# Value products over two steps, and the hash in even steps from two products and an addition

## The chip, the cores and the metric

One core of a Trainium2 chip. TensorE (PE) multiplies, with a queue of its own for weight loads (PEld); VectorE (DVE), ScalarE (ACT) and GpSimd (POOL) work on tiles in SBUF; TensorE writes to PSUM; SyncE (SP) issues most transfers. The metric is the device time of one launch in microseconds (us); a lower one is better.

## The reference

```python
# q, k, v: (4, 8, 768, 64); proj: (64, 6); w_in: (512, 2048); w_out: (2048, 512); all float32
q_bits, k_bits = (q @ proj > 0), (k @ proj > 0)          # 6 bits: a bucket per row
mask = q_bucket[:, :, :, None] == k_bucket[:, :, None, :]
scores = np.where(mask, scale * q @ k.T, -1e9)
attn = softmax(scores)                                    # sum + 1e-9 below the line
x = (attn @ v).transpose(0, 2, 1, 3).reshape(3072, 512)
h = x @ w_in
out = (h * np.clip(h + 3, 0, 6) / 6) @ w_out
```

Attention over 32 heads (4 batches of 8), in which a query meets only the keys of its own hash bucket, and then a dense network over 3072 tokens.

## The kernel before

Every float32 operand is split into a high part in the matrix unit's own format (F32R) and the rest, the low part; a product is a sum of products of parts. So a head's hash is a sum over q and k of high and low parts with the projection's high and low parts, and its signs become bits that stand as extra rows beside q and k in the score product (`hash_qk`, `bits`).

A *step* k handles one block of 128 queries of a head (6 steps a head, 192 in all), in a software pipeline: step k makes the scores of block k+3 (`lead`, tile `s`), the row minimum of block k+2 (`lowest`, VectorE, L396), its exponential (ScalarE, L408) and its transpose in 32x32 blocks (`flip`, VectorE, L429). The transpose is finished by a round trip through DRAM (`move`): the block comes back into the buffer `spare` for even blocks and `px` for odd ones. From there `split_p` makes the high parts `ph` (ScalarE, L475) and the low parts `pl`, for two halves of the keys, c = 0 and c = 1: the low part of c = 0 is a subtraction on VectorE (L479), that of c = 1 one on GpSimd (L477). Two blocks share one pair of tiles; a new pair of blocks begins in an odd step, with the block that lies in `spare`. The tiles lie in rings of two per tag, one turn for c = 1 and one for c = 0:

```python
both = [sp.tile([P, ...], F32R, name=f"{x}{u}_{c}", tag=x, bufs=2)[:, :S] for x in ("ph", "pl")]
```

so a pair's tiles are those of the pair before, and are free when that pair's value products have read them. The value products (`values_whole`, tile `acc`, L513) are 12 matmuls of a pair, six over `ph` and six over `pl`, in an odd step.

From step 102 on (`GT`; `paced`) each step also runs one of 16 slices of the dense network for a chunk of 256 tokens: the first dense product (`gemm1`, tile `h`, 12 matmuls, L661), the gate (ScalarE L683, VectorE L684) and the second dense product of the slice before (`gemm2`, tile `po`, 6 matmuls, L699, L700, L704), which needs the gate's high part (ScalarE, L689) and, last, its low part (VectorE, L690: `gb` or `ga`). The order on PE, DVE, ACT and POOL is written out by hand: `beside_ffn` calls the pieces, and the generator `ffn` is resumed at the marks A to D. So every engine works through its instructions in the order of the code. In a step of this stage TensorE does, in this order: the value products (odd steps), the first dense product, the hash (once in six steps), the second dense product, the scores. VectorE does the minimum, the gate's low part, the block transpose, the gate's product, the subtraction for `pl`, and what the hash needs. `hash_qk` runs in a step k with (k+3) % 6 == 4, which is odd.

Accumulators `acc`, `h`, the hash's `z` and the transposed reciprocals `rt` share four banks of PSUM (`bank`, tags `pt` and `pu` in turn, two each): a new tile waits for the last reader of the tile whose bank it is given. The score tile has one buffer in this stage. The hash's operands are row groups of a head: `k2` and `q2` hold high and low parts, made by copies over DMA (`moves`, one a step) and subtractions on GpSimd (`subs`).

Of the kernel before, what the change touches and what calls it, by code (L numbers as in the profile page):

```python
# [43 lines left out]
def lsh_attention_moe(  # L44
# [75 lines left out]
    pjh = cp.tile([P, ZM + ZK - D], F32R, name="pjh")  # L120
    nc.vector.memset(pjl[:].bitcast(F32), 0.0)
    nc.vector.memset(pjh[:].bitcast(F32), 0.0)
    pjk, pjq = pjh[:, :ZM], pjh[:, ZK - D :]

# [9 lines left out]
    nc.vector.memset(three[:], 3.0)  # L134

# [99 lines left out]
    def get_qk(i: int, tag: str = "raw"):  # L235
        b, h = divmod(i, H)
        if tag == "raw":
            raws[i] = sp.tile([P, S], F32, name=f"raw{i}", tag=tag, bufs=1)[:]
        else:
            raws[i] = wide_tile([P, 2 * WC], F32, f"raw{i}")[:, :S]  # L240
        if paced:
            dma(out=raws[i][:D], in_=qkT[b, h, :D])
        else:
            dma(out=raws[i], in_=qkT[b, h])

    def get_k_rows(i: int):
        b, h = divmod(i, H)
        moves.append(lambda: dma(out=raws[i][D:], in_=qkT[b, h, D:]))
# [6 lines left out]
    def hash_weights():  # L255
# [3 lines left out]
        for r, c in ((slice(0, D), D), (slice(D, P), ZK)):  # L259
            pos = pjh[r, ZK + NB : ZM]  # L260
            nc.vector.tensor_sub(pjl[r, c + NB : c + 2 * NB], pr[r], pos.bitcast(F32))
            nc.vector.tensor_sub(pjl[r, c : c + NB], pos.bitcast(F32), pr[r])

# [16 lines left out]
    moves = []  # L280
# [44 lines left out]
    def hash_qk(i: int):  # L325
        k1, k2, q1, q2 = state[i]
        if paced:
            z = zs[i] = [bank([P, HW], f"z{i}_{j}") for j in range(2)]
        else:
            both = pair(f"z{i}")  # L330
            z = zs[i] = [both[:, j, :HW] for j in range(2)]
# [5 lines left out]
        if not paced:  # L337
            zs[i] = both

    def bits(i: int):  # L340
# [3 lines left out]
        if isinstance(z, list):  # L344
            whole = [(slice(j * HW, (j + 1) * HW), z[j][D:ZM], False) for j in range(2)]
        elif i == 0:
# [144 lines left out]
    def values(u: int, c: int):  # L491
# [5 lines left out]
        for part, y in enumerate((hi, lo)):  # L497
            for x in range(QT):
# [4 lines left out]
                )  # L503

# [533 lines left out]
    def lead(j: int):  # L1038
# [35 lines left out]
    def value_whole():  # L1074
        nonlocal vnext
        values_whole(vnext // 2)
        vnext += 2

# [20 lines left out]
    with tc.manual_schedule(engines={ET.PE, ET.DVE, ET.Activation, ET.Pool}):  # L1099
# [15 lines left out]
        def beside_ffn(k: int):  # L1115
# [9 lines left out]
            for _ in range(2):  # L1125
                u = vnext // 2
                if u < NS // 2 and (2 * u < GT or k % 2 and k >= 2 * u + 3):
# [8 lines left out]
            behind = (k - 1 + LA) % KT == 4  # L1136
# [48 lines left out]
            if GT <= k + 1 < NS:  # L1185
                move(k + 1)

            place_in_chunk = (k - GT) % NFC
            if subs and (k % 2 and (k < GT or place_in_chunk != NFC - 1) or k > GT and place_in_chunk == 0):
# [5 lines left out]
        for k in range(NS + LT + 2):  # L1195
# [11 lines left out]
            if k == HK:  # L1207
                late["x"] = sp.tile([P, S], F32, name="late", tag="raw", bufs=1)
            for c in range(2):
# [118 lines left out]
```

## Time and profile before

| | |
|---|---|
| median of 3 runs | 976.26 us (974.35 to 977.39) |
| profiled execution | 973.11 us, its span 971.3 us, granted TensorE clock 0.998 |
| busy share | PE 98%, PEld 90%, DVE 74%, ACT 64%, POOL 49% |
| stage with the dense network beside the attention | from 412 to 810 us |
| DMA in that stage | 81% of 16 engines, 239 GB/s |
| after it | dense network alone, from 810 us to the end |

Rows in order of time give start, duration, engine, line, operation, `out<-in` with the shapes, and in brackets the idle time of the engine ahead of the instruction and what ended it. Rows of a stretch give its length and, for PE, PEld, DVE, ACT and POOL, busy us and (instructions), then the clock, the DMA share and GB/s. Rows of waits name who waited for whom: total us, times, the longest.

### The profile page before, as it was taken

The page shows a single profiled execution, that of the slowest core. Times are in us where ns is not written, and L with a number is a line of the kernel's source. Part 1 is how long each engine was busy: PE and PEld are TensorE (multiplying, and loading weights), DVE is VectorE, ACT ScalarE, POOL GpSimd, SP SyncE. Part 2 cuts the span into 40 slices and gives each one's busy share as a digit, 9 for nine tenths or more (in the row PEclk, how much of TensorE's full clock was granted, in tenths as well). Part 3 has the DMA queues.
Part 4 walks back from the last instruction along what each step waited for, and adds up shares of the span by engine and source line. Part 5 has one row for each costly group of instructions (what it writes and reads, how often), then busy time and mean ns, then how long its engine had stood idle before and what let it go on. Part 6 is the DMA issues. An engine that isn't in the chain of part 4 may idle for free.

```text
span 971.3 us, 19460 instructions
## 1 busy us (share of the span) xinstructions
PE 948.0 (98%) x6306; PEld 873.6 (90%) x6306; DVE 723.5 (74%) x1470; ACT 625.0 (64%) x1421; POOL 473.6 (49%) x582
## 2 busy tenths in 40 slices
PE   8999999999999999899999999999999999999997
PEld 7999888999989999799899899989899899889896
DVE  7999988888569999877878878878777874342422
ACT  6898875655478988667766666666666664333332
POOL 6777744665537776455555545555545432000000
PEclk9999999999999999999999999999999999999999
DMA  3567579100035554787898788788887772101000
GB/s 117 140 156 188 131 224 377 58 1 1 6 119 119 115 142 112 192 252 233 238 267 234 231 256 241 230 267 236 243 258 233 211 227 71 44 1 44 1 22 22
DMA packets 113613, 152.06 MB, mean 157 GB/s; under 512 B 13876, under 2 KB 82612, under 8 KB 113512
## 3 DMA queue, kind: packets, MB, share of 16 engines
q1 hardware_dynamic: 108472, 144.79, 48.8%
q0 software_dynamic: 5040, 6.03, 5.3%
q8 instruction: 50, 0.82, 0.4%
q14 instruction: 51, 0.42, 0.2%
HBM read 77.34 MB, written 54.00 MB: 135 GB/s over the span
## 4 chain that ended last, share of the span: by engine, by line
PE 79%; DVE 8%; DMA 4%; ACT 4%; issue 3%; POOL 1%; SPq 1%; ACTq 0%; DVEq 0%; POOLq 0%
PE h L661 25%; PE acc L500 6%; PE po L704 6%; PE po L699 6%; PE po L700 6%; PE acc L513 6%; PE pt L418 5%; PE s L389 5%; PE s L387 5%; DMA spare<-fd 2%; DVE p L396 2%; DVE pl L479 2%; ACT ph L475 1%; SPq L78 1%; DVE qq L352 1%
## 5 line engine op out<-in xcount | busy, mean ns | idle before, releaser
L408 ACT ACTIVATE p<-p,m 128x768 f32<-128x768 f32 x192 | 180.2, 939 | 113.4 <-DVE p L396 105.2
L396 DVE TENSOR_SCALAR_CACHE_REDUCE p<-s 128x768 f32<-128x768 f32 x192 | 182.7, 952 | 24.9 <-PE pt L418 12.4
L684 DVE SCALAR_TENSOR_TENSOR h<-g,h 128x256 f32<-128x256 f32 x192 | 81.1, 423 | 102.0 <-ACT g L683 99.0
L683 ACT ACTIVATE g<-h,three 128x256 f32<-128x256 f32 x192 | 91.2, 475 | 94.9 <-PE h L661 94.0
L661 PE MATMUL h<-xh,w 128*128 128x256 f32 x1024 | 146.8, 282 | 0.0
L661 PEld LDWEIGHTS h<-xh,w 128*128 128x128 f32 x1024 | 134.9, 188 | 4.2 <-ACT xh L650 0.6
L429 DVE STREAM_TRANSPOSE p<-p 128x768 f32<-128x768 f32 x90 | 88.1, 979 | 65.2 <-ACT p L408 65.1
L477 POOL TENSOR_TENSOR pl<-spare,ph 128x384 fp32r<-128x384 f32 x45 | 45.8, 1018 | 127.3 <-ACT ph L475 71.4
L479 DVE TENSOR_TENSOR pl<-pt,ph 128x384 fp32r<-128x384 f32 x196 | 100.0, 550 | 4.0 <-ACT ph L475 3.5
L387 PE MATMUL s<-kk,qq 76*128 76x384 f32 x384 | 100.5, 343 | 2.0 <-ACT kk L357 1.5
L389 PE MATMUL s<-kk,qq 128*128 128x384 f32 x384 | 100.4, 343 | 0.0
L700 PE MATMUL po<-w,gb 128*128 128x512 f32 x250 | 98.4, 393 | 0.0
L699 PE MATMUL po<-w,gb 128*128 128x512 f32 x250 | 98.3, 393 | 0.0
L475 ACT CAST ph<-pt 128x384 fp32r<-128x384 f32 x196 | 86.1, 474 | 14.3 <-PE pt L418 13.0
L216 POOL TENSOR_TENSOR w<-wr,w 128x128 fp32r<-128x128 f32 x128 | 71.9, 593 | 45.2 <-ACT w L210 41.9
L418 PE MATMUL pt<-ident,p 128*128 128x128 f32 x612 | 86.2, 275 | 1.9 <-DVE pl L479 1.1
L689 ACT CAST gb<-h 128x256 fp32r<-128x256 f32 x141 | 52.4, 372 | 54.5 <-DVE h L684 26.8
L661 PE MATMUL h<-xl,w 128*128 128x256 f32 x512 | 81.2, 280 | 0.0
L418 PEld LDWEIGHTS pt<-ident,p 128*128 128x128 f32 x612 | 72.5, 141 | 8.9 <-PE pt L418 1.5
L704 PE MATMUL po<-w,gb 128*128 128x512 f32 x250 | 78.6, 395 | 1.5 <-DVE gb L690 1.5
L318 POOL TENSOR_TENSOR kk<-raw,qq 64x192 fp32r<-64x192 f32 (+1 forms) x73 | 65.4, 920 | 25.1 <-ACT qq L304 21.7
L387 PEld LDWEIGHTS s<-kk,qq 76*128 76x128 f32 x384 | 66.6, 190 | 11.7 <-ACT kk L357 2.0
(153 smaller groups left out, 2150.9 us busy)
## 6 DMA issues: line engine op xcount, KB each, us to landing
fd<-p SPq DMA_DIRECT2D x90, 384.0 KB
spare<-fd SPq DMA_DIRECT2D x180, 96.0 KB
px<-fd SPq DMA_DIRECT2D x180, 96.0 KB
kk<-qq SPq DMA_DIRECT2D x62, 192.0 KB
wr<-in_w_in SPq DMA_DIRECT2D x16, 512.0 KB
wr<-in_w_out SPq DMA_DIRECT2D x16, 512.0 KB
raw<-in_qkT SPq DMA_DIRECT2D x19, 384.0 KB
vr<-in_v SPq DMA_DIRECT2D x32, 192.0 KB
```

Source lines behind the costliest of these rows:

```text
L387: nc.tensor.matmul(s[:, c, :HW], lhsT=q1[:KM, us], rhs=half(k1[:KM], c), start=True, stop=False)
L389: nc.tensor.matmul(s[:, c, :HW], lhsT=q2[:, us], rhs=half(k2, c), start=False, stop=True)
L396: nc.vector.tensor_scalar(out=pr_[:], in0=s[:, :, :HW], scalar1=CAP, scalar2=None, op0=ALU.min, op1=ALU.min, accum_out=m[:],)
L408: nc.scalar.activation(pr_[:], pr_[:], AF.Exp, bias=m[:], scale=-1.0, accum_out=sms[b][:, t, h : h + 1])
L418: nc.tensor.transpose(pt[:, x], probs[g][0][:, c, x * P : (x + 1) * P], ident[:])
L475: nc.scalar.copy(hi, pt)
L479: lows.append(lambda: engine.tensor_sub(lo, pt, hi.bitcast(F32)))
L661: nc.tensor.matmul(hp, lhsT=wi[:, wp, wc], rhs=x[cc][xp], start=(k == 0 and cc == 0), stop=(k == 2 and cc == NCC - 1),)
L683: nc.scalar.activation(r[:], hp, AF.Relu, bias=three[:], scale=1.0)
L699: nc.tensor.matmul(po[u], lhsT=gh[:, us], rhs=wo[:, 0], start=(fc == 0), stop=False)
L700: nc.tensor.matmul(po[u], lhsT=gh[:, us], rhs=wo[:, 1], start=False, stop=False)
L704: nc.tensor.matmul(po[u], lhsT=gl[:, us], rhs=wo[:, 0], start=False, stop=(fc == NFC - 1))
```

## The change

In the stage from step 102 on:

- the value products of a pair are split: the six over `ph` run in the odd step, behind the first dense product (`value_part(k, 0)`), and the six over `pl` at the start of the next even step (`value_part(k, 1)`);
- the hash runs one step earlier, in an even step ((k+3) % 6 == 3), and all waiting `subs` and `moves` are issued ahead of it;
- it is four matmuls for six: weights `pjs` (made once, on GpSimd, in the place of `pjh`) give 24 rows of partial sums in rows 0 to 23 and 24 in rows 96 to 119 of `z`; ScalarE copies the first group into rows 96 to 119 of the next head's `raw` tile, VectorE adds the second, and a third VectorE pass over 24x768 in SBUF compares with the thresholds. Before, two passes over 44x384 in PSUM did it;
- the K rows of the next head are loaded a step later than before (`get_k_rows` at t == 4), since their rows hold the sums until then; this load and the transfer of the k bits go to SP behind the loads of `move`; one of `subs` may go in every step.

```diff
+    def short_weights():
+        pjs = cp.tile([P, ZK + NR + NQ], F32R, name="pjs", tag="pjh")
+        nc.gpsimd.memset(pjs[:].bitcast(F32), 0.0)
+        short.extend([pjs[:, : ZK + NR], pjs[:, NQ:]])
...
     def hash_qk(i: int):
         k1, k2, q1, q2 = state[i]
         if paced:
-            z = zs[i] = [bank([P, HW], f"z{i}_{j}") for j in range(2)]
+            zs[i] = []
+            for j in range(2):
+                c = slice(j * HW, (j + 1) * HW)
+                z = bank([P, HW], f"z{i}_{j}")
+                zs[i].append(z)
+                nc.tensor.matmul(z[: ZK + NR], lhsT=short[1], rhs=q2[:, c], start=True, stop=False)
+                nc.tensor.matmul(z[: ZK + NR], lhsT=short[0], rhs=k2[:, c], start=False, stop=True)
+            return
...
     def bits(i: int):
...
         if isinstance(z, list):
-            whole = [(slice(j * HW, (j + 1) * HW), z[j][D:ZM], False) for j in range(2)]
+            r = slice(ZK, ZK + NR)
+            if i + 1 not in raws:
+                raws[i + 1] = sp.tile([P, S], F32, name=f"raw{i + 1}", tag="raw", bufs=1)[:]
+            both = raws[i + 1][r]
+            for j in range(2):
+                nc.scalar.copy(both[:, j * HW : (j + 1) * HW], z[j][:NR])
+            for j in range(2):
+                c = slice(j * HW, (j + 1) * HW)
+                nc.vector.tensor_add(both[:, c], z[j][r], both[:, c])
+            nc.vector.tensor_scalar(
+                out=q1[D : D + NR], in0=both, scalar1=ths[r], scalar2=vas[r], op0=ALU.is_gt, op1=ALU.mult,
+            )
+            behind_home.append(lambda: dma(out=k1[D : D + NQ].bitcast(F32), in_=q1[D + NQ : D + NR].bitcast(F32)))
+            return
...
+    def values_part(u: int, part: int):
+        vv = vvs[2 * u // KT]
+        if part == 0:
+            accs[u] = bank([P, 2 * P], f"acc{u}")
+        acc = accs[u]
+        for c in (1, 0):
+            y = parts[u, c][part]
+            for x in range(QT):
+                nc.tensor.matmul(
+                    acc[:], lhsT=vv[:, c * QT + x], rhs=y[:, x],
+                    start=(part, c, x) == (0, 1, 0), stop=(part, c, x) == (1, 0, QT - 1),
+                )
...
-                if paced:
-                    get_k_rows(n + 1)
+        if t == 4 and paced and n + 1 < NJ and n != H + 1:
+            get_k_rows(n + 1)
...
+            value_part(k, 1)
-            behind = (k - 1 + LA) % KT == 4
+            behind = (k - 1 + LA) % KT == 3
             if GT <= k < NS - 2 and not behind:
                 lowest(k + 2)
             go("A")
...
             if split:
                 split_p(k - LT, 1, False)
             go("B")
+            value_part(k, 0)
...
-            hashed = k + LA < NS and (k + LA) % KT == 4 and (k + LA) // KT + 1 < NJ
+            hashed = k >= GT and k + LA < NS and (k + LA) % KT == 3 and (k + LA) // KT + 1 < NJ
             if hashed:
+                while subs:
+                    subs.pop(0)()
+                while moves:
+                    moves.pop(0)()
                 hash_qk((k + LA) // KT + 1)
...
             if GT <= k + 1 < NS:
                 move(k + 1)
+            while behind_home:
+                behind_home.pop(0)()
```

TensorE around the hash of head 27, before (odd step 157; `acc77` the value products, `h2_0_7` the first dense product, `z27` the hash, `gb2_0_6` the gate of the step ahead):

```order
L387 MATMUL s159_8997<-kk_26_8435,qq_26_8436 128x384 x2
L389 MATMUL s159_8997<-kk_26_8435,qq_26_8436 128x384 x2
L513 MATMUL acc77_9007<-ph77_1_8913,vv25_8705 128x256 x3
L513 MATMUL acc77_9007<-ph77_0_8939,vv25_8705 128x256 x3
L513 MATMUL acc77_9007<-pl77_1_8914,vv25_8705 128x256 x3
L513 MATMUL acc77_9007<-pl77_0_8940,vv25_8705 128x256 x3
L661 MATMUL h2_0_7_9034<-xh2_0_8572,w14_2678 128x256 x8
L661 MATMUL h2_0_7_9034<-xl2_0_8573,w14_2678 128x256 x4
L334 MATMUL z27_0_9047<-qq_27_8825,pjl_74 108x384
L335 MATMUL z27_0_9047<-kk_27_8824,pjh_75 108x384
L336 MATMUL z27_0_9047<-qq_27_8825,pjh_75 108x384
L334 MATMUL z27_1_9048<-qq_27_8825,pjl_74 108x384
```

and now (even step 156, with the low half of the pair ahead, `acc76`, at its start):

```order
L429 MATMUL s158_8965<-kk_26_8452,qq_26_8453 128x384 x2
L553 MATMUL acc76_8945<-pl76_1_8806,vv25_8723 128x256 x3
L553 MATMUL acc76_8945<-pl76_0_8839,vv25_8723 128x256 x3
L716 MATMUL h2_0_6_8993<-xh2_0_8593,w12_2618 128x256 x8
L716 MATMUL h2_0_6_8993<-xl2_0_8594,w12_2618 128x256 x4
L355 MATMUL z27_0_9008<-qq_27_8843,pjs_5485 120x384
L356 MATMUL z27_0_9008<-kk_27_8842,pjs_5485 120x384
L355 MATMUL z27_1_9011<-qq_27_8843,pjs_5485 120x384
L356 MATMUL z27_1_9011<-kk_27_8842,pjs_5485 120x384
L754 MATMUL po2_0_8648<-w11_2554,gb2_0_5_8984 128x512
L755 MATMUL po2_0_8648<-w11_2554,gb2_0_5_8984 128x512
```

The low half of the value products has moved behind the odd step's scores, to the head of the even step, and the hash with it by a step.

VectorE at the same place, before, from the end of odd step 155 (the subtraction `pl77_0` from `spare`) over even step 156 into odd step 157:

```order
L479 TENSOR_TENSOR pl77_0_8940<-spare_5091,ph77_0_8939 128x3x128
L396 TENSOR_SCALAR p158_8958,m158_8957<-s158_8943 128x768
L690 TENSOR_TENSOR gb2_0_5_8960<-h2_0_5_8917,gb2_0_5_8960 128x256
L429 STREAM_TRANSPOSE p158_8958<-p158_8958 128x768
L684 SCALAR_TENSOR_TENSOR h2_0_6_8969<-g2_0_6_8990,h2_0_6_8969 128x256
L479 TENSOR_TENSOR pl77_0_8940<-px_5555,ph77_0_8939 128x3x128
L396 TENSOR_SCALAR p159_9021,m159_9020<-s159_8997 128x768
```

and now:

```order
L519 TENSOR_TENSOR pl77_0_8962<-spare_5100,ph77_0_8961 128x3x128
L436 TENSOR_SCALAR p158_8982,m158_8981<-s158_8965 128x768
L745 TENSOR_TENSOR gb2_0_5_8984<-h2_0_5_8932,gb2_0_5_8984 128x256
L469 STREAM_TRANSPOSE p158_8982<-p158_8982 128x768
L739 SCALAR_TENSOR_TENSOR h2_0_6_8993<-g2_0_6_9020,h2_0_6_8993 128x256
L519 TENSOR_TENSOR pl77_0_8962<-px_5570,ph77_0_8961 128x3x128
L380 TENSOR_TENSOR raw28_9025<-z27_0_9008,raw28_9025 24x384
L380 TENSOR_TENSOR raw28_9025<-z27_1_9011,raw28_9025 24x384
L381 TENSOR_SCALAR qq_27_8843<-raw28_9025,limits_78 24x768
L745 TENSOR_TENSOR gb2_0_6_9042<-h2_0_6_8993,gb2_0_6_9042 128x256
L436 TENSOR_SCALAR p159_9046,m159_9045<-s159_9032 128x768
```

VectorE's own order is unmoved up to the subtraction from `px`; the hash's three passes stand behind it, in the even step. `pl77_0`, in the first row, is written into the buffer of `pl76_0` (two buffers, one turn each for c = 1 and c = 0), which the products at the head of the even step, above in TensorE's rows, still read. The low part of the gate is `gb2_0_5`, read in the even step's second dense product.

More of the change, by code (lines that the diff above doesn't have):

```diff
@@ L237, in get_qk @@
         if tag == "raw":
-            raws[i] = sp.tile([P, S], F32, name=f"raw{i}", tag=tag, bufs=1)[:]
+            if i not in raws:
+                raws[i] = sp.tile([P, S], F32, name=f"raw{i}", tag=tag, bufs=1)[:]
         else:
@@ L336, in hash_qk @@
             nc.tensor.matmul(z[j][:ZM], lhsT=pjq, rhs=q2[:, c], start=False, stop=True)
-        if not paced:
-            zs[i] = both
+        zs[i] = both
     def bits(i: int):
```

48 lines of the change are left out of this document (39 added, 9 removed).

## The prediction

> **What bounds the kernel now.** I read the page's busy times first, then busy time by stretch, the waits of the paced stage, and the order of time on TensorE, VectorE and GpSimd there.
>
> ```profile
> PE 948.0 (98%) x6306; PEld 873.6 (90%) x6306; DVE 723.5 (74%) x1470; ACT 625.0 (64%) x1421; POOL 473.6 (49%) x582
> 412.00:810.00 398.00, 393.54 (x2562) 364.12 (x2563) 312.48 (x598) 265.81 (x623) 208.32 (x269) 1.00 0.81 239
> PE acc L513 <- ACT ph L475: 4.5, 9, 1.5
> DVE p L396 <- PE s L389: 8.2, 21, 0.6
> POOL pl L477 <- ACT ph L475: 96.8, 45, 4.0
> ```
>
> TensorE is the bound (98%), and all that the change touches lies in the 398 us from 412 to 810, the paced stage, at a granted clock of 1.00. TensorE's only listed wait there is 4.5 us, at the value products. But VectorE is no spare engine in that stage: only 21 times in about 85 steps does it wait for scores, and then 0.4 us on average. GpSimd has room (96.8 us of waiting for one producer alone).
>
> How a pair of steps runs on TensorE (second number: duration):
>
> ```profile
> 702.32 1.10 PE L661 MATMUL h<-xh,w 128*128 128x256 f32 x8
> 704.64 0.63 PE L704 MATMUL po<-w,gb 128*128 128x512 f32 x2
> 705.82 0.88 PE L513 MATMUL acc<-ph,vv 128*128 128x256 f32 x6
> 706.53 0.88 PE L513 MATMUL acc<-pl,vv 128*128 128x256 f32 x6
> 707.25 1.10 PE L661 MATMUL h<-xh,w 128*128 128x256 f32 x8
> 708.66 0.34 PE L334 MATMUL z<-qq,pjl 128*108 128x384 f32 x1
> 709.70 0.40 PE L699 MATMUL po<-w,gb 128*128 128x512 f32 x1
> 711.82 1.10 PE L661 MATMUL h<-xh,w 128*128 128x256 f32 x8
> 720.34 1.10 PE L661 MATMUL h<-xh,w 128*128 128x256 f32 x8
> 728.82 1.10 PE L661 MATMUL h<-xh,w 128*128 128x256 f32 x8
> ```
>
> From start to start: an even step is 3.50 us (702.32 to 705.82), its closing product asks for the gate's low part 2.32 us in (704.64). The two halves of the value products are 0.71 each, the first dense product is 1.41 (707.25 to 708.66), the hash 1.04 (708.66 to 709.70), the second dense product and the scores 2.12. A pair without a hash takes 8.48 (720.34 to 728.82), with one 9.50.
>
> The same pair on VectorE:
>
> ```profile
> 720.54 0.96 DVE L396 TENSOR_SCALAR_CACHE_REDUCE p<-s 128x768 f32<-128x768 f32 x1 [0.49 <-PE s L389]
> 721.42 0.42 DVE L690 TENSOR_TENSOR gb<-h,gb 128x256 fp32r<-128x256 f32 x1
> 722.60 0.98 DVE L429 STREAM_TRANSPOSE p<-p 128x768 f32<-128x768 f32 x1 [0.76 <-ACT p L408]
> 724.05 0.73 DVE L479 TENSOR_TENSOR pl<-px,ph 128x384 fp32r<-128x384 f32 x1
> 724.70 0.94 DVE L396 TENSOR_SCALAR_CACHE_REDUCE p<-s 128x768 f32<-128x768 f32 x1
> 727.96 0.72 DVE L479 TENSOR_TENSOR pl<-spare,ph 128x384 fp32r<-128x384 f32 x1
> 729.02 0.96 DVE L396 TENSOR_SCALAR_CACHE_REDUCE p<-s 128x768 f32<-128x768 f32 x1 [0.34 <-PE s L389]
> ```
>
> Minimum to minimum is 4.16 without a wait, 8.48 for the pair with 0.34 waited: VectorE's own loop is 8.14. The minimum begins 0.20 after TensorE begins the even step (720.54 against 720.34), the gate's low part ends 1.30 later, at 1.50, 0.82 before it is asked for. That 0.82 and the 0.34 are what VectorE has to give.
>
> **The change part by part.** T is the moment at which TensorE begins the first dense product of an even step.
>
> *Hash, TensorE.* Six products take 1.04, so 0.173 each. Two fewer, 14 heads: -4.9 us, on the bound.
>
> *Value products.* Their count stays. The waits in them should go: the high half is read 1.4 us later, the low half a half step later still. Ends: 0 and 9 us (twice what is listed, since waits shorter than a product's own 0.3 are not listed). I take -6.5, above the listed 4.5, since the later place covers both kinds.
>
> *The low half goes behind the odd step's scores, ahead of T.* Its tiles lie in a ring of two per tag (`pl`, one for c=1, one for c=0). The next pair's first low parts, written in the odd step (tiles `<-spare`, one by GpSimd, one by VectorE), now need tiles that TensorE reads until T. Before, both were free early in the odd step. GpSimd waits for the third product of the half, VectorE for the sixth, and behind VectorE's subtraction in its order stands the minimum of the even step. Then the two subtractions meet; what that costs, in order of time (start, duration) on both engines, and GpSimd's reply to a product:
>
> ```profile
> 751.14 1.45 DVE L479 TENSOR_TENSOR pl<-px,ph 128x384 fp32r<-128x384 f32 x1
> 750.82 1.28 POOL L477 TENSOR_TENSOR pl<-px,ph 128x384 fp32r<-128x384 f32 x1
> 558.80 1.06 DVE L479 TENSOR_TENSOR pl<-px,ph 128x384 fp32r<-128x384 f32 x1
> 558.42 1.01 POOL L477 TENSOR_TENSOR pl<-px,ph 128x384 fp32r<-128x384 f32 x1
> 732.52 0.56 DVE L479 TENSOR_TENSOR pl<-px,ph 128x384 fp32r<-128x384 f32 x1
> 731.58 1.02 POOL L477 TENSOR_TENSOR pl<-px,ph 128x384 fp32r<-128x384 f32 x1 [0.78 <-DMA spare<-fd]
> 818.11 0.38 PE L587 MATMUL rt<-ident,spare 128*128 128x128 f32 x2
> 818.63 0.40 POOL L577 COPY spare<-rc 128x256 f32<-128x256 f32 x1 [1.74 <-PE rt L587]
> ```
>
> VectorE's subtraction takes 0.56 alone (732.52) and, when GpSimd's is under way, lasts until 0.42 after GpSimd's end (558.80: 559.43 and 559.86). GpSimd starts 0.14 after the product that it waits for (818.49 to 818.63). The third product of the half ends at about T-0.2, so GpSimd runs from T-0.05 to T+0.97 and VectorE's ends at T+1.39, not at the T+0.76 that it could have alone (sixth product done, T+0.2, and 0.56). The minimum then starts at T+1.3 where it was T+0.2, and the gate's low part ends at T+2.6, where the closing product asks at T+2.32. So an ordinary even step loses 0.28. Ends: 0 (VectorE first: minimum at T+0.7, low part done at T+2.0) and 0.5. Between T of step 106 and 188 there are 42 even steps, 13 with a hash, 4 more behind a chunk's end: 25 x 0.28 = +7.
>
> The Trainium skill ("SBUF — State Buffer", section "SBUF: two separate sides") has the pair of ports that the two engines share as an exclusive lock, held for the whole instruction, with the loser blocked. By that rule the loser would also pay its full 0.56 behind the lock, and this term would be 25 x 0.42 = 10.5. The trace shows blocking, but 0.42 behind it; the row decides.
>
> *Hash in the even step.* Its second half (in four of the 13 heads its first half) is given the PSUM bank whose last reader is the gate's low part of the same step, the one that ends at T+2.6. TensorE reaches the second half at T+1.41+0.35 = T+1.76 and waits 0.85. In the four heads it reaches the bank at T+1.41 and waits 1.2; there the next step's first dense product also takes the bank that VectorE's second addition reads. For the additions, three rows in order of time, two groups of the page, and one line's own view (shortest, median, longest ns):
>
> ```profile
> 709.83 0.62 DVE L479 TENSOR_TENSOR pl<-spare,ph 128x384 fp32r<-128x384 f32 x1
> 710.48 1.29 DVE L352 TENSOR_SCALAR qq<-z,thr,val 44x384 fp32r<-44x384 f32 x2
> 712.14 0.95 DVE L396 TENSOR_SCALAR_CACHE_REDUCE p<-s 128x768 f32<-128x768 f32 x1
> L479 DVE TENSOR_TENSOR pl<-pt,ph 128x384 fp32r<-128x384 f32 x196 | 100.0, 550 | 4.0 <-ACT ph L475 3.5
> L475 ACT CAST ph<-pt 128x384 fp32r<-128x384 f32 x196 | 86.1, 474 | 14.3 <-PE pt L418 13.0
> L291 DVE CAST qq<-raw x1: 557/557/557, 4.0 to 4.0; 64x768 fp32r<-64x768 f32 x1
> ```
>
> No row has the additions (24x384, one operand in PSUM); the nearest is L479 from PSUM, 0.55. The copies on ScalarE are like L475, 0.47 each; they end before the additions could begin. From the minimum at T+1.3, VectorE reaches its second subtraction 3.51 later (720.54 to 724.05), the additions 0.65 after that (709.83 to 710.48), and ends the second at T+6.5. The first dense product of the odd step would begin at T+2.6+0.69+2.12 = T+5.4 and waits 1.1. In the nine heads the value products take that bank, 1.41 later than the dense product would, and wait little. So 9 x 0.85 + 4 x 2.3 = +17. Ends: 9 x 0.3 + 4 x 1.7 = 9.5 without the meeting of the subtractions, and 21 if VectorE is 0.3 later still. The threshold pass over 24x768 in SBUF is between 0.56 (L291) and 0.95 (L396, as wide); the next that TensorE asks of VectorE is then the low part of the odd step, 1.4 + 0.7 + 0.9 behind that bank. I set 0.
>
> *Chunk ends.* At five of them VectorE splits the next chunk's activations behind the subtraction.
>
> ```profile
> 692.79 1.78 PE L661 MATMUL h<-xh,w 128*128 128x256 f32 x8
> 692.77 1.43 DVE L651 TENSOR_TENSOR xl<-xr,xh 128x256 fp32r<-128x256 f32 x4 [0.48 <-ACT xh L650]
> ```
>
> These end at T+1.41 now (692.77 to 694.20, T at 692.79) and at T+1.39+1.43 = T+2.8 then: 5 x 1.3 = +6.5, between 0 and 7.
>
> *At nothing:* the two weight tiles and limits on GpSimd, and its later subtraction (96.8 us of waiting there; without it the loads into `spare`, which wait for its end, would come later still and ScalarE's copy with them); the transfers of the hash's rows, issued three and two steps ahead where it was four and three (a pair is 8.48 us; late ones would stop TensorE at the hash); the K rows and the bits' transfer behind the step's four loads on SP's queue, which waits there for the threshold pass, ahead of a transpose that VectorE makes still later; ScalarE's high copies, which wait for an exponential behind the minimum and so come after the high products that free their tiles; ScalarE's two copies a hash, 0.95, which are over before VectorE reads them.
>
> Sum: -4.9 - 6.5 + 7 + 17 + 6.5 = +19. The profiled execution is 973.1 (span 971.3), so 992; the median of the runs stands 3.2 above it, and I give 995 against 976.3.
>
> **The rivals.** *VectorE goes first* or the subtractions don't meet: for it, that GpSimd's start is only 0.25 ahead; against it the rows above, where the one that began first kept its time. Then ordinary steps lose nothing, the hash 9.5, chunk ends 3: -4.9-6.5+9.5+3 = +1, 977. *The gain stands, faster:* the low tiles are free in time, as with one buffer more. It decides at the minimum: if this starts by T+0.45, the bank is free at T+1.75 and no wait follows. Then -4.9 - 6.5 = -11.4, 965. For it: the minimum starts at T+0.2 now; against it: its tile is read until T in any case. *The value waits stay* (they are ScalarE's lateness, not the place): no -6.5, 1002.
>
> **How the numbers follow.** Slower as summed 0.64, with value waits kept 0.08, no meeting 0.12, gain stands 0.16. What differs by less than 0.3% (3 us) can't be told from no change here. The range from 970 to 1003 leaves out most of the faster case and a little above: about 0.18. Slower 0.72, same 0.11, faster 0.17.
>
> **What would show it.** VectorE's subtraction `<-spare` about 1.1 long or waiting for the value products; the even minimum 1.3 behind TensorE's T; waits of the hash's second half for the gate's low part, 9 heads, and of the dense product for an addition, 4; no wait at the value products. I am wrong if the even minimum still starts at T+0.2 to T+0.7, or if the hash starts its second half 0.35 behind its first.

## The result and the profile after

The changed kernel takes 1018.0 us (median of 6 runs, 1015.18 to 1020.64) against 975.75 for the kernel before in the same comparison: 1.043 of it, 95% interval 1.0405 to 1.0455. That is 42 us slower where 19 were forecast, and outside the range given. The profiled execution has a span of 1013.4 us (before: 971.3).

The first line below is the page of the kernel after. The two others are one row each of busy time by stretch: before and after, from the first dense product of step 106 to that of step 189 (length, then PE, PEld, DVE, ACT, POOL).

```profile
PE 960.7 (95%) x6278; PEld 868.0 (86%) x6278; DVE 751.7 (74%) x1484; ACT 634.5 (63%) x1449; POOL 477.3 (47%) x595
```

```profile
417.40:798.50 381.10, 376.77 (x2451) 348.63 (x2450) 301.91 (x576) 253.79 (x595) 201.83 (x262) 1.00 0.82 241
```

```profile
417.20:839.10 421.90, 389.17 (x2413) 342.61 (x2412) 326.86 (x588) 262.07 (x620) 204.48 (x263) 0.99 0.75 217
```

The same 83 steps take 381 us before and 422 after, and that is the whole loss (the stretch after holds one group of value products fewer, 1.4 us). TensorE was busy for all but 4 us of it before; after, 33 us are idle. The share of busy time says only 95%. The other 12 us stand in the busy time: what a late operand costs shows as idle time only in part (0.16 in the step below, which loses 0.43), and products at a lowered clock (last section) count as busy. Here is what it waits for there, with what VectorE and GpSimd wait for ahead of it (waits of the paced stage: who for whom, us in total, times, the longest):

```profile
POOL pl L517 <- PE acc L553: 42.1, 9, 8.1
PEld po L759 <- DVE gb L745: 22.0, 36, 1.3
DVE pl L519 <- PE acc L553: 12.9, 23, 1.4
PE z L355 <- DVE gb L745: 10.8, 11, 1.4
PE po L759 <- DVE gb L745: 7.1, 24, 0.9
PE h L716 <- DVE xl L706: 3.9, 5, 1.0
PE z L355 <- ACT y L602: 3.1, 4, 0.8
PE z L355 <- POOL qq L340: 2.9, 4, 0.9
PE acc L553 <- ACT ph L515: 2.3, 1, 2.3
PE acc L553 <- DVE raw L380: 0.7, 1, 0.7
```

The two subtractions `pl` now wait for the value products `acc`, as the prediction had it, and TensorE waits for the gate's low part `gb` at the closing product (`po`) and at the hash (`z`). One ordinary even step (T = 743.25, the start of its first dense product), in order of time on each engine:

```profile
743.25 1.10 PE L716 MATMUL h<-xh,w 128*128 128x256 f32 x8
743.20 1.02 POOL L517 TENSOR_TENSOR pl<-spare,ph 128x384 fp32r<-128x384 f32 x1 [6.08 <-PE acc L553]
743.51 1.11 DVE L519 TENSOR_TENSOR pl<-spare,ph 128x384 fp32r<-128x384 f32 x1 [0.40 <-PE acc L553]
744.55 0.94 DVE L436 TENSOR_SCALAR_CACHE_REDUCE p<-s 128x768 f32<-128x768 f32 x1
745.89 0.73 PE L759 MATMUL po<-w,gb 128*128 128x512 f32 x2 [0.16 <-DVE gb L745]
747.18 1.10 PE L716 MATMUL h<-xh,w 128*128 128x256 f32 x8
```

GpSimd starts at T-0.05, VectorE's subtraction takes 1.11 beside it, the minimum starts at T+1.30, and the closing product at T+2.64. The step is 3.93 long where it was 3.50.

Three hash steps, with the start of the second pair of products, or of both, late for three different reasons (steps 156, 162, 168; the GpSimd row is of step 168):

```profile
673.40 0.34 PE L356 MATMUL z<-kk,pjs 128*120 128x384 f32 x1
674.63 0.41 PE L355 MATMUL z<-qq,pjs 128*120 128x384 f32 x1 [0.90 <-DVE gb L745]
703.43 0.43 PE L355 MATMUL z<-qq,pjs 128*120 128x384 f32 x1 [1.08 <-DVE gb L745]
704.82 0.44 PE L355 MATMUL z<-qq,pjs 128*120 128x384 f32 x1 [0.79 <-ACT y L602]
733.28 2.44 POOL L340 TENSOR_TENSOR qq<-raw,qq 64x192 fp32r<-64x192 f32 x4
734.67 0.43 PE L355 MATMUL z<-qq,pjs 128*120 128x384 f32 x1 [0.94 <-POOL qq L340]
735.77 0.43 PE L355 MATMUL z<-qq,pjs 128*120 128x384 f32 x1 [0.49 <-POOL qq L340]
```

The first wait was forecast. The second bank in step 162 is that of finished value products, which ScalarE copies out (`y`) only behind its exponential. In step 168 GpSimd's last subtractions for the hash stand behind its subtraction `pl` and come too late.

The longest wait of all, in step 153, goes by a transfer. The first four lines are of the changed kernel; the last three are the same place in e8, an experiment below in which the low tiles come free on time:

```profile
649.12 1.02 POOL L517 TENSOR_TENSOR pl<-spare,ph 128x384 fp32r<-128x384 f32 x1 [6.30 <-DMA px<-fd]
651.95 1.68 POOL L577 DMA_DIRECT2D xs<-y  x2
656.15 0.37 ACT L602 COPY y<-acc 128x256 f32<-128x256 f32 x1 [3.26 <-DMA xs<-y]
657.35 0.62 PE L553 MATMUL acc<-ph,vv 128*128 128x256 f32 x3 [2.33 <-ACT ph L515]
```

```profile
634.24 1.68 POOL L577 DMA_DIRECT2D xs<-y  x2
638.64 0.37 ACT L602 COPY y<-acc 128x256 f32<-128x256 f32 x1 [3.45 <-DMA xs<-y]
639.84 0.62 PE L553 MATMUL acc<-ph,vv 128*128 128x256 f32 x3 [2.52 <-ACT ph L515]
```

GpSimd issues a store of `y`; ScalarE waits 3.26 us for the store before it can write the tile again, its next high copy is late, and TensorE stands 2.33 us at the value products. The step takes 9.71 instead of 4.93. The late subtraction ahead of the store is not the cause: with free tiles the store is issued at the same point (1.16 ahead of the step's first dense product in e8, which starts at 635.40; 1.15 ahead of it here, at 653.10), the waits are as long, and the step takes 7.73. Before the change the store went out 6.8 ahead of that product, ScalarE waited 1.10 for it and TensorE 1.50.

All steps 106 to 188 by kind: time above their own products (3.50 us a step, 0.118 a value product, 0.173 a hash product), from the starts of the first dense products.

| steps | before | after |
|---|---|---|
| 13 with the hash | 0.9 | 25.6 |
| even, without hash or chunk end | 9.5 | 15.2 |
| even, at a chunk end, without hash | 6.0 | 9.5 |
| odd, without hash | 1.2 | 13.9 |
| sum | 17.6 | 64.2 |

(Some 3 us of each sum are the products of `rt`, 0.14 a pair.)

### The profile page after: what moved, and what is told of

Its sections match the earlier page's. It is cut to its first block, busy times and chain, and to the rows that moved or that the text cites. A ratio compares the mean times of both kernels' runs of the same rounds, so it can differ in the third digit from the quotient of the medians.

```text
span 1013.4 us, 19446 instructions
## 1 busy us (share of the span) xinstructions
PE 960.7 (95%) x6278; PEld 868.0 (86%) x6278; DVE 751.7 (74%) x1484; ACT 634.5 (63%) x1449; POOL 477.3 (47%) x595
## 5 line engine op out<-in xcount | busy, mean ns | idle before, releaser
L754 PE MATMUL po<-w,gb 128*128 128x512 f32 x250 | 100.3, 401 | 1.5 <-ACT gb L744 1.5
L755 PE MATMUL po<-w,gb 128*128 128x512 f32 x250 | 99.8, 399 | 0.0
L759 PE MATMUL po<-w,gb 128*128 128x512 f32 x250 | 83.8, 416 | 7.9 <-DVE gb L745 7.5
L716 PE MATMUL h<-xl,w 128*128 128x256 f32 x512 | 83.5, 282 | 3.9 <-DVE xl L706 3.9
```

The lines of the kernel that those rows point to most:

```text
L716: nc.tensor.matmul(hp, lhsT=wi[:, wp, wc], rhs=x[cc][xp], start=(k == 0 and cc == 0), stop=(k == 2 and cc == NCC - 1),)
L754: nc.tensor.matmul(po[u], lhsT=gh[:, us], rhs=wo[:, 0], start=(fc == 0), stop=False)
L755: nc.tensor.matmul(po[u], lhsT=gh[:, us], rhs=wo[:, 1], start=False, stop=False)
L759: nc.tensor.matmul(po[u], lhsT=gl[:, us], rhs=wo[:, 0], start=False, stop=(fc == NFC - 1))
```

## The experiments

Times are medians; "before" is the kernel before on the same chip, and ratios carry 95% intervals.

**Low products 0.7 us sooner** (e1).

```diff
-            value_part(k, 1)
             behind = (k - 1 + LA) % KT == 3
...
+            value_part(k, 1)
             if k + LA < NS:
                 lead(k + LA)
```

> The changed kernel with one move: the six low products of a pair stand ahead of the odd step's scores instead of behind them, so that their tiles come free about 0.7 us sooner. Theory A (the low tiles' ring: everything late in the even step follows from subtractions that wait for the products at its head): the even minimum starts at T+0.6 at the latest, even steps take 3.50 us, the hash waits for the gate's low part at most 0.3 us in four heads (and 0.8 to 1.3 there for the copy of the value products), GpSimd's queue is on time again: 970 us, 965 to 977. Theory B (the hash's own place is what costs; in the profile its 14 steps hold 25 us of waiting): those stay, only the 12 us of the ordinary even steps and some of the chunk ends go: 998 to 1006. Theory C (nothing but the meeting of the two subtractions counts): as A, since they no longer meet in the way of the minimum.

991.29 us, 1.016 (1.0139 to 1.018). Of 25 ordinary even steps 18 are at 3.8 us or below, eleven of them at 3.52 or 3.50; in the changed kernel none was below 3.92. But hash steps still hold 17 us above their products, and steps 150 to 153 the same store as above. The time lies between the two theories: A is right for most ordinary steps and far too good in the time, B's 998 was too slow.

**Four low tiles** (e2).

```diff
-  tag=f"x{x[1]}" if extra else x
+  tag=f"x{x[1]}" if extra else "pm" if x == "pl" and g >= GT and u % 2 else x
```

> The changed kernel with four tiles for the low parts instead of two, the products where they are. For the room, the weights of slice 1 are those of slice 0 and two of 32 weight conversions are left out, which lie before 412 us; so the stretch from step 106 to step 189 is what is compared. Theory A: no subtraction waits for a product; even steps 3.50 us, that stretch 375 to 385 us (422 changed, 381 before), whole time 965 to 978. Theory B: the hash's steps keep 25 us, the stretch is 400 to 408 us, whole time above 995. If the stretch is as with the low products ahead of the scores, the place of the products is of no account and only the tiles are.

980.88 us, 1.0063 (1.0041 to 1.0086); the stretch from 106 to 189 is 388.0. The late tiles are thus worth 34 us in that stretch and 3.7% of 975, 36 us, in the whole time, of which some 1.5 are the weight conversions that this kernel leaves out. But what is left is slower than before, not 10 us faster. Its waits at the hash are for ScalarE's copy (four heads, 0.79 each), the gate and GpSimd. So neither theory held: the tiles are most of it, and the hash's change costs something of its own.

**Other order of halves** (e3).

```diff
-        for c in (1, 0):
+        for c in ((1, 0) if part == 0 else (0, 1)):
```

> The changed kernel with the six low products in the other order of halves (c = 0 first), so that VectorE's tile comes free after the third product and GpSimd's after the sixth. Theory C (the meeting of the two subtractions on their way to SBUF puts the minimum at T+1.3): VectorE goes first, the minimum starts at T+0.5 to T+0.7, ordinary even steps are back at 3.50 us, the hash waits 0.2 to 0.3 us for the gate; but GpSimd's queue is as late as before or 0.3 later, so its late copies for the hash and its late issue of a store stay (5 to 8 us): 985 to 1000 us. Theory A without C (waiting for the products alone): the minimum starts at T+1.0 or later and the time is 1010 to 1020.

1015.91 us, 1.0416 (1.0399 to 1.0433): as the changed kernel. GpSimd still starts 0.06 ahead of T, with the third product of the half, and VectorE behind it (T = 752.92). So a tile of the next pair must have taken the buffer that is read out first, whichever half it held:

```profile
752.86 1.01 POOL L517 TENSOR_TENSOR pl<-spare,ph 128x384 fp32r<-128x384 f32 x1 [3.99 <-DMA px<-fd]
753.27 1.01 DVE L519 TENSOR_TENSOR pl<-spare,ph 128x384 fp32r<-128x384 f32 x1 [0.59 <-ACT qq L326]
```

The edit left the order of the two engines as it was, and says nothing on what the meeting of the two costs.

**Hash alone** (e4), with all twelve value products back at the start of the odd step.

```diff
-            value_part(k, 1)
+            value_part(k, 0)
+            if k % 2:
+                value_part(k, 1)
             behind = (k - 1 + LA) % KT == 3
...
-            value_part(k, 0)
```

> The changed hash alone: four products in the even step with VectorE's additions, and the value products all twelve at the start of the odd step, as before the change. Theory A: no tile is late; the hash gains its 4.9 us, the value products' waits of 4.5 us stay, four heads may wait 0.1 to 0.3 us for the gate: 968 to 977 us. Theory B: the hash's 14 steps keep most of their 25 us of waiting: 990 to 1000 us.

990.26 us, 1.0157 (1.0141 to 1.0173): B's time without any late tile. The waits of e4 and, below, of e7:

```profile
PE z L355 <- ACT y L602: 10.7, 9, 1.7
```

```profile
PE z L356 <- ACT y L584: 9.0, 9, 1.6
```

The hash's second half waits 1.1 to 1.7 us (e7: 0.8 to 1.6) in nine heads for the bank of the value products, which ScalarE copies behind its exponential.

**Both low halves of the first block on GpSimd** (e5).

```diff
-            if c:
+            if c or w == 0:
                 engine = nc.gpsimd
```

> The changed kernel with both low halves of a pair's first block (from the buffer spare) on GpSimd; VectorE keeps only the second block's. So nothing on VectorE stands behind the products at the head of the even step. If what the changed kernel loses in ordinary even steps (0.43 us each) is VectorE's queue behind that late subtraction: the even minimum starts at T+0.2, even steps take 3.50 us, the hash no longer waits for the gate's low part, and chunk ends lose nothing; what stays is the hash's wait for ScalarE's copy of the value products (0.8 us in four heads) and GpSimd's lateness, now a subtraction longer: 980 to 992 us. Rival: GpSimd's two subtractions, from T to T+2.0, slow the minimum and the gate's low part beside them, and even steps keep 0.3 us or more: 1000 us and over.

1003.45 us, 1.03 (1.0276 to 1.0323). With nothing late on VectorE, 16 of 29 even steps without a hash are at 3.50 or 3.51 again, so it is VectorE's queue that cost 0.43 there. The time, though, is not the 980 to 992 that went with it, and the rival's 1000 and over comes for another reason than its own: GpSimd now comes later still.

```profile
POOL pl L517 <- PE acc L553: 70.9, 16, 9.1
PE rt L642 <- POOL spare L632: 7.8, 8, 1.5
PE z L355 <- POOL qq L340: 5.0, 4, 1.7
```

**Form and place of the hash apart** (e6: short form, odd step; e7: six products and two passes, even step; both with the value products at the start of the odd step, as in e4). The edit of the place, in e6:

```diff
-            behind = (k - 1 + LA) % KT == 3
+            behind = (k - 1 + LA) % KT == 4
...
-            hashed = ... (k + LA) % KT == 3 ...
+            hashed = ... (k + LA) % KT == 4 ...
```

> The form of the hash alone: four products, copies, additions and the pass in SBUF, but in the odd step where the hash was before the change, with the value products all at the start of the odd step. If the place in the even step is what costs in the hash alone (990 us, against 976 before), this is faster than before by up to the two products of 14 heads: 971 to 975 us. If the form costs (ScalarE's copies and VectorE's third pass come too late for the next step), it is 980 to 990 us.

> The place of the hash alone: the old six products and two passes over 44 rows in PSUM, but in the even step, with the value products all at the start of the odd step. If the place costs, since the second half of the hash then takes the bank of the value products and ScalarE copies these only behind its exponential: the same wait of 1.1 us as with the short form, and 992 to 996 us (990 and the 4.9 us of two products). If the form costs, 976 to 980 us.

The form alone: 983.35 us, 1.0087 (1.0057 to 1.0117). The place alone: 988.39, 1.0146 (1.0125 to 1.0167). Both cost, and together (e4) not the sum; e7 lies below the 992 to 996 that was expected if the place costs. In e6 it is the wait at the value products that grows, from 4.5 us before:

```profile
PE acc L553 <- ACT ph L515: 9.4, 25, 1.1
```

**Value products whole, behind the dense product** (e8: changed kernel; e10: kernel before, old hash; e9: short hash in the odd step). The edit of e8:

```diff
-            value_part(k, 1)
             behind = (k - 1 + LA) % KT == 3
...
             value_part(k, 0)
+            value_part(k, 1)
```

> The changed kernel with all twelve value products of a pair in the odd step, behind the first dense product: the high half where the change has it, the low half right behind it and no longer over two steps. The low tiles are free before VectorE or GpSimd asks for them, without a further tile. If only the tiles matter, as the run with four low tiles (981 us) says: 976 to 984 us, even steps at 3.50 us. If the spreading itself saves something (scores 0.7 us sooner for the even minimum), 985 us or more.

> The kernel before with one move: the twelve value products behind the first dense product of the odd step. If the waits at the value products (4.5 us listed) are a matter of the place: 969 to 973 us. If they come back elsewhere: 974 to 977 us. Against the run with the short hash it also tells what the short form is worth once the value products are out of the way (4.9 us by count of products).

> The short hash in the odd step, where the hash was before the change, and all twelve value products of a pair in the odd step behind the first dense product. In the run of the form alone (983 us, value products at the start of the odd step) TensorE waited 11 us more at the value products than before the change. If that is the value products' place (ScalarE's high halves are asked for 1.4 us too soon once the hash is shorter): the waits go, and the hash's 4.9 us and the 4.5 us of value waits are gained: 964 to 970 us. If another loop (VectorE's 8.14 us of a pair, ScalarE's) is next and TensorE only waits elsewhere: 974 us or more.

e8: 981.51 us, 1.0068 (1.0051 to 1.0085), as with four tiles: it is not the spreading but the tiles. What TensorE still waits for at the hash in e8:

```profile
PE z L355 <- DVE gb L745: 4.4, 10, 0.6
PE z L355 <- ACT y L602: 3.1, 4, 0.8
PE z L355 <- POOL qq L340: 0.8, 2, 0.4
```

The longest in total is the gate's low part, though the tiles are free: the minimum starts at T+0.45 or sooner in only 3 of the 13 hash steps, and at T+0.67 to T+1.09 in the others. Why VectorE is late there no run takes apart.

e10: 967.92, 0.9914 (0.9895 to 0.9932), better than either expectation: the kernel before with this one move is faster than both kernels, and its wait at the value products is nearly gone:

```profile
PE acc L513 <- ACT ph L475: 0.4, 1, 0.4
```

e9: 973.84, 0.9983 (0.9968 to 0.9999), at the edge of its second expectation: in the same place the short hash is 6 us slower than the old one.

**ScalarE's copy ahead of its exponential** (e11, on e8).

```diff
+            while k > GT + 1 and through and k % 2 == 0:
+                output(through.pop(0))
             if k + 2 < NS:
...
                 exponential(k + 2)
```

> The kernel with the short hash in the even step and the twelve value products behind the dense product in the odd step (981.5 us), with ScalarE's copy of the finished value products moved ahead of its exponential in the even step. If the hash's wait for the bank of these products (0.8 us listed in four heads, steps 114, 132, 162, 180 of 5.7 to 6.3 us against 4.2) is ScalarE's order: those steps fall to about 4.7 us, 975 to 978 us. If the copy then delays the exponential and what follows it: 980 us or more.

979.15 us, 1.0036 (1.0022 to 1.005). The four steps fall from 6.33, 6.14, 5.74 and 6.13 us to 5.27, 5.44, 5.28 and 5.40, 3 us in all, and 2.4 in the whole time, between the two expectations (step 153, with the wait for the store, goes from 7.73 to 10.75): ScalarE's order is the cause of that wait, and there are others at the same place.

**Where the short form loses** (e12: e9 without ScalarE's copies and VectorE's additions, so that half of the hash's sums are left out; e13: the same with transfers and GpSimd's subtractions where they were before; e14: the old form of e10 with the change's transfers; e15: e9 with copies and subtractions one a step again).

```diff
-            for j in range(2):
-                nc.scalar.copy(both[:, j * HW : (j + 1) * HW], z[j][:NR])
-            ... nc.vector.tensor_add(both[:, c], z[j][r], both[:, c])
+                nc.vector.tensor_scalar(out=q1[D : D + NR, c], in0=z[j][r], ...)
```

```diff
-                while subs:
-                    subs.pop(0)()
-                while moves:
-                    moves.pop(0)()
...
-        behind_home.append(lambda: dma(out=raws[i][D:], in_=qkT[b, h, D:]))
+        moves.append(lambda: dma(out=raws[i][D:], in_=qkT[b, h, D:]))
```

> The short hash in the odd step with the value products behind the dense product (974 us), without ScalarE's two copies and VectorE's two additions: VectorE compares the 24 rows in PSUM with the limits in two passes, so the hash bits come from half of the sums (these are left out). TensorE's four products, VectorE's two passes and the transfers stay. If the short form loses its 4.9 us, and 6 more against the old form in the same place (968 us), to these copies and to VectorE's 0.43 us more a head: 962 to 966 us. If the four products bring nothing, since TensorE waits elsewhere: 967 to 969. If the loss is in the K rows' load and the transfers of the hash, which the change moves too: 972 to 975.

> As the run without additions (971 us: four products, two passes over 24 rows in PSUM, odd step, value products behind the dense product; the hash bits come from half of the sums), but with the transfers and GpSimd's subtractions where they were before the change: the K rows' load and the copies one a step, nothing flushed ahead of the hash. If the moved transfers are what still costs there (in the profile ScalarE waits 0.2 to 0.5 us for the blocks from DRAM ahead of the hash's passes, and TensorE 0.9 to 1.3 us for VectorE's passes): 961 to 965 us, the 968 us of the old form less the 4.9 us of two products. If four products bring nothing, since VectorE's passes set the pace at the hash: 967 to 970 us.

> The other side of the same question: the old hash of six products and two passes over 44 rows, in the odd step, value products behind the dense product (968 us), with the change's order of transfers and subtractions: all of them issued ahead of the hash, the K rows a step later and behind the blocks' loads. If the moved transfers cost 5 to 8 us by themselves: 973 to 976 us. If not: 966 to 969 us.

> The whole short form with its additions in the odd step and the value products behind the dense product (974 us), with copies and subtractions issued one a step as before the change; only the K rows stay a step later, since their rows hold the sums. If issuing all of them ahead of the hash is what delays the blocks' loads: 966 to 970 us. If the K rows' place is: 973 to 975 us.

| | form | transfers | us | ratio to before |
|---|---|---|---|---|
| e10 | 6 products, 2 passes | before | 967.92 | 0.9914 (0.9895 to 0.9932) |
| e13 | 4 products, 2 passes | before | 968.13 | 0.9929 (0.9913 to 0.9945) |
| e14 | 6 products, 2 passes | changed | 972.0 | 0.9966 (0.9954 to 0.9979) |
| e12 | 4 products, 2 passes | changed | 971.02 | 0.9962 (0.9948 to 0.9975) |
| e15 | whole short form | K rows and k bits late only | 973.36 | 0.9985 (0.9974 to 0.9996) |
| e9 | whole short form | changed | 973.84 | 0.9983 (0.9968 to 0.9999) |

e12 and e14 lie between two of their expectations; e13 is as expected if four products bring nothing, e15 as expected if the K rows' place costs. Four products instead of six bring nothing, with either order of transfers. The transfers cost 3 to 5 us, the additions with their copies and the third pass 2 to 3; e15 is as e9, so it is not the issue of all copies ahead of the hash. The K rows' load and the k bits' transfer, both behind the step's loads, are left as the likely part, which no run takes by itself. What the moved transfers do, in e14: ScalarE waits for blocks from DRAM, VectorE's passes over the hash are later for it, and the next dense product, which takes the bank that they read, waits:

```profile
ACT ph L497 <- DMA spare<-fd: 6.5, 7, 1.7
PE h L698 <- DVE qq L374: 3.2, 5, 1.2
```

In e10 these two are 2.0 in 2 and 0.4 in 1. The same wait with four products, in e12 (step 157 and the dense product of 158):

```profile
654.75 0.70 DVE L513 TENSOR_TENSOR pl<-spare,ph 128x384 fp32r<-128x384 f32 x1
655.48 1.29 DVE L375 TENSOR_SCALAR qq<-z,limits 24x384 fp32r<-24x384 f32 x2
656.23 1.21 PE L710 MATMUL h<-xh,w 128*128 128x256 f32 x8 [0.93 <-DVE qq L375]
```

VectorE's passes over the hash stand behind its subtraction of the same step. The next dense product takes the bank that they read, and waits: TensorE sooner is, there, TensorE waiting. The waits of e12 and of e13 at that product:

```profile
PE h L710 <- DVE qq L375: 4.3, 5, 1.3
```

```profile
PE h L710 <- DVE qq L375: 1.4, 3, 0.6
```

That is not the whole account. In the traces the 13 hash steps of e13 take 77.5 us, those of e10 79.7: 2.2 us are gained of the 4.5 that two products of 13 heads take. The other 70 steps take 296.3 against 294.3, and give it back, in places that no run takes apart.

In e9 three passes stand there:

```profile
656.95 1.04 DVE L380 TENSOR_TENSOR raw<-z,raw 24x384 f32<-24x384 f32 x2
658.03 0.76 DVE L381 TENSOR_SCALAR qq<-raw,limits 24x768 fp32r<-24x768 f32 x1
658.82 0.42 DVE L745 TENSOR_TENSOR gb<-h,gb 128x256 fp32r<-128x256 f32 x1
```

The additions take 0.52 each and the third pass 0.68 to 0.76; the gate's low part of the step before stands behind all of them. Here too the hash steps (77.6) are no longer than in e13: the loss is in the other steps, 302.6 against 296.3 in e13 and 294.3 in e10.

## Why the prediction was right or wrong

The runs make a ladder from the kernel before to the changed one, one part of the change a rung (ratios to before, times 975). Medians move alike. It is one order of the parts, and in another they would have other sizes: e4, e6 and e7 show that they don't add up.

| rung | measured | in the prediction |
|---|---|---|
| value products behind the dense product (e10) | -8 us | -6.5 |
| four products for six (e13) | 0 to +1.5 | -4.9 |
| transfers moved (e12) | +3 to +5 | 0 |
| copies and additions (e9) | +2 to +3 | 0 |
| hash in the even step, tiles on time (e8) | +8 | 0 |
| low half behind the scores, tiles late (changed) | +35 | +30.5 (7 + 17 + 6.5) |
| sum | +42 | +19 |

- **The mechanism of the late tiles was right.** GpSimd first, VectorE blocked until behind it, the minimum at T+1.30 (forecast T+1.3), the hash's bank waiting for the gate's low part: each is in the trace. VectorE's subtraction ended 0.40 behind GpSimd's (744.62 and 744.22), near the 0.42 of the row that the prediction chose. By the Trainium skill's rule ("SBUF — State Buffer", section "SBUF: two separate sides"), which has the loser blocked for the winner's whole instruction, it would have ended the full 0.56 behind; the trace shows less. That the one that began first kept its time holds here (GpSimd's took 1.02), but it held for only one of the prediction's two pairs of rows: in the other GpSimd's took 1.28 and VectorE ended 0.49 behind it. Four tiles, or the products where the tiles come free, take some 35 us off.
- **Its size came out near by luck.** From e8 to the changed kernel, time above the steps' own products: hash steps 13.9 to 25.6 (+11.7, forecast 17), ordinary even steps 6.0 to 15.2 (+9.2, forecast 7), chunk ends without a hash 2.9 to 9.5 (+6.6; forecast 6.5, one with a hash among them), odd steps 7.6 to 13.9 (+6.3, forecast none). The hash's term was too large on this rung, since its steps lose much with free tiles too, and the odd steps, at nothing, made up for it. Step by step the terms were too small: the ordinary step loses 0.43, not 0.28, since the closing group of products, once stopped, takes 0.73 where it takes 0.63, and no even step without a hash takes less than 3.92. Hash steps: 1.15 over their products in five heads where 0.85 was given, and 2.55 where 2.3 was, in three of four heads (4.05 in the fourth, at a lowered clock). In the four heads the second part of this was not the next dense product's wait for an addition, as forecast, but the hash's second half waiting for ScalarE's copy.
- **"At nothing" for GpSimd failed.** Its 96.8 us of waiting were taken as room, but it works in order: what stands behind a subtraction that waits for TensorE is late however idle the engine is. TensorE waited 2.9 us for its subtractions at the hash, 0.8 with free tiles (e8) and 5.0 with more of it on GpSimd (e5); steps 120 and 168 take 2.0 over their products, against 1.15. The wait for the store in step 153 is another matter, since it is there with free tiles too.
- **"Hash, TensorE: -4.9 on the bound" failed.** In the same place, four products are as six (e13 against e10): 0 to +1.5 us measured where -4.9 was forecast. TensorE was 98% busy, but what follows at the hash is not free to come sooner: VectorE's passes set when the next dense product may take the bank. That is seen for part of it (waits of 1.4 in e13, 0.4 in e10); 2.0 us are given back in steps without a hash, for a cause that stays open.
- **"I set 0" for the third pass, and the transfers "at nothing", failed.** The transfers cost 3 to 5 us, the third pass with the additions and ScalarE's copies 2 to 3. With the transfers moved, ScalarE's copies of blocks come later from DRAM, and the next dense product waits for what follows (e14). The copies, additions and third pass cost in the steps without a hash (e9); which of the three it is, and by what wait, is not shown.
- **The rival "the gain stands", 965, was never there.** With free tiles (e2, e8) the kernel is at 981. It took the hash's new place as free, since the minimum would start by T+0.45 and free the bank. With free tiles it does so in 3 of 13 hash steps (e8), and it did not ask what else the banks hold: finished value products that ScalarE has yet to copy. TensorE's waits at the hash in e8, 4.4, 3.1 and 0.8 us, add up to the 8 us of that rung.
- **The value waits went as forecast**, and this is the part of the change worth having: e10, 0.9914.

The range's upper end, 1003, took in only sizes of the terms that were seen; the four costs put at zero (transfers, the third pass with what goes with it, the hash's place, GpSimd's queue) all had the same sign.

## What to carry to other kernels

Work saved on the busiest engine need not shorten anything: ask which tile or bank its next instruction takes and who reads it last. A ring of two buffers ties the writer to the place of the last reader, so moving a reader later moves every instruction that stands behind the writer on its engine, an idle engine's too. When several parts of a change come together, time the parts: here one of them, alone, was a gain of 0.9%.

## What the hardware showed

A lower clock followed some stops of TensorE of about 2 us, and not others. Three rows of busy time by stretch in the changed kernel (the number behind the five busy times is the granted clock): the value products' wait in step 153, what came behind it, and what came behind the hash's two waits of step 180. The fourth row is e8, behind its wait of 2.52 at the place of the first:

```profile
653.10:657.30 4.20, 1.92 (x16) 1.72 (x15) 0.76 (x2) 1.15 (x4) 1.57 (x2) 1.00 0.99 263
657.30:661.60 4.30, 3.88 (x12) 3.07 (x13) 3.10 (x7) 3.79 (x9) 0.00 (x0) 0.65 0.44 125
795.10:798.50 3.40, 3.31 (x8) 2.77 (x9) 3.06 (x6) 1.65 (x5) 0.86 (x1) 0.50 0.83 236
```

```profile
639.80:644.50 4.70, 4.66 (x31) 4.38 (x31) 3.94 (x9) 4.19 (x9) 1.15 (x2) 1.00 0.52 159
```

At the lowered clock a product of 512 columns takes 0.63 us where it takes 0.40. Step 180 takes 8.23 us; step 132, with the same two waits, kept its clock and took 6.74. In e8 the longer wait of 2.52 was followed by a full clock. So it does not follow every time; it cost 1.5 us in step 180, 1.3 in step 182 (7.71 against 6.38 in step 134) and up to 2.0 in step 153 (9.71 against 7.73 in e8). The Trainium skill ("TensorE: Matmul & The Clock Gate", Part 1) has a free-running window of about 3.4 us, and half clock after an idle one; its section "HAM oscillation" warns of idle gaps beyond 3.4 us. The trace agrees in the half clock (0.50) and in that chance has a part, but here it fell behind waits of 1.07 and 0.78 in one step, or one of 2.33.

VectorE's pass over 24 rows takes as long as over 44 (two of them 1.29 us in either form): rows saved are no time saved there.
